# Two-half matmuls on one core: the halves take turns at the accumulation banks

## The chip, the core and the metric

The kernel runs on one core of a Trainium2 chip. The metric is the device time of one execution in microseconds; the median of three runs is given. Engines are named as in the profile: PE (TensorE; PEld its weight loads), DVE (VectorE), ACT (ScalarE), POOL (GpSimd), SP (SyncE, which here issues the transfers).

## The reference, cut to what matters

```python
# 8192 tokens (2 x 4096), 192 features, 8 heads, 7 taps
w = softmax(weight_gen, axis=-1)                  # per token and head
y[s, h] = sum_k w[s, h, k] * x_padded[s + k, h]   # causal convolution
h1 = silu(y @ w_gate) * (y @ w_val)               # 192 -> 1536
z = h1 @ w_out                                    # 1536 -> 192
h2 = z @ w_in                                     # 192 -> 2048
out = (h2 * clip(h2 + 3, 0, 6) / 6) @ w_out2      # 2048 -> 192
```

## The kernel before

The tokens are worked on in 16 tiles of 512. A tile passes four stages: softmax and convolution on DVE and ACT (`conv_items`, whose last sums are lines 360 and 361; for tiles 0 and 1 PE adds the taps, `conv_pe_items`); transposes on PE, which put features on the partitions (`transposes`); the first layer in 12 blocks of 128 hidden columns (kind 1: `m1_in`, `m1_ew`, `m1_out`); and the second layer in 8 blocks of two times 128 (kind 2: `m2_in`, `m2_ew`, `m2_out`). Softmax comes for two tiles at a time. Products of float32 accuracy are made of three: each operand is split into a high and a low part on ACT and DVE (`gsplit`, lines 571 and 666; for transposed input line 526, for a first-layer result lines 584 to 586).

PE's array is used as two halves of 64 rows (`HALVES`), each of which can run a matmul of its own beside the other; two such matmuls are called a pair here. The 192 features are three chunks of 64. In `in_proj` half 0 adds all three chunks into one bank (pg, or the first ph) and half 1 all three into another (pv, or the second ph): 9 pairs. Each half reads the input in its own partitions, so chunks 0 and 1 are needed in both: `s0` holds them, `s1` is a copy with the halves exchanged, made by two transfers (`swap`, line 432), and `s2` holds chunk 2 twice (`double`). A tile's three input tiles come from a ring of four sets (`alloc_split`).

Accumulation uses eight banks: four for in-projections (pool `hp`), which the transposes share, and four (`acc_bank`). The first-layer out-projection of tiles 0 and 1 is five matmuls on the full array, into two banks; for later tiles (`m1_out_halves`) it is five pairs into four banks, two for each half, which the evacuation (`evacuate`, lines 631 to 641) copies and adds. The second-layer out-projection is 16 pairs in four rounds over four banks; the halves work two banks apart, and a bank changes hands behind a mark, a one-element memset on POOL (line 695), which the matmul that takes the bank waits for.

Instructions are issued in the order in which the code is written. Block by block it is: in-projection of block b, out-projection of an earlier block (`pend`, `drain`), elementwise work of block b on ACT and DVE; convolution and weight conversion are filled in between up to a budget in ns (`take`). An evacuation (`urgent`) is put ahead of the next block's elementwise work (`run_urgent`). Tiles 0 and 1 share their first-layer blocks, while the weights are loaded as 64-bit words and converted (`convert_stream`; `i_part` loads a chunk in two transfers of 64 partitions and rounds it in line 255). Then come the first layers of tiles 2 and 3, and from there second layer of tile t and first layer of tile t + 3 in turn. `to_pe(t + 3)`, the wait for the convolution and the transposes, stands in block 4 of a second-layer phase.

## Time and profile before

| | before |
|---|---|
| median of 3 runs | 1319.44 us (1318.07 to 1319.69) |
| profiled execution, its span | 1317.99 us, 1316.2 us |
| PE busy | 1264.0 us, 96% |
| DVE, ACT, POOL busy | 70%, 52%, 4% |
| moved by DMA | 64.01 MB |

The busy shares say which engine is full, and the chain of waits which work, followed back from the end, set it. Windows give the busy time of a stretch, and the timeline the instructions in it, each with the idle time of its engine just before and what ended that. `PE 64*128` marks a matmul on half of the array; starts of the pairs, not their lengths, tell how fast they follow, since they overlap.

### The profile page before, as it was taken

Reading aid. Unit: us, or ns where it says so; the run is one execution under the profiler, and the core shown is the slowest. Engines: PE = TensorE matmul, PEld = TensorE weight load, DVE = VectorE, ACT = ScalarE, POOL = GpSimd, SP = SyncE. Lnnn points to the kernel's source line nnn. Section 1 sums busy time; section 2 is a strip of 40 time slices with the busy share of each in tenths; the row PEclk is TensorE's granted clock in tenths of the full one; section 3 lists DMA queues with packets and bytes.
Section 4 is the critical chain, followed back from the end, with each engine's and each line's share of the span. In section 5 each row is a group of like instructions: output and inputs, shape, how many; then the busy total and the mean of one; then the engine's idle time right before and its main releaser. Section 6 shows DMA issues by size and latency. Waiting matters only on the chain.

```text
span 1316.2 us, 29560 instructions
## 1 busy us (share of the span) xinstructions
PE 1264.0 (96%) x11992; PEld 1085.9 (83%) x11992; DVE 927.3 (70%) x1500; ACT 686.1 (52%) x1204; POOL 48.3 (4%) x515
## 2 busy tenths in 40 slices
PE   5899798999999999999999999999999999999998
PEld 5666576799798897979888798988979898887998
DVE  5797685698677776777767676777767777655655
ACT  3354454566474544646365454746446463644655
POOL 1000000000000000000000000000000000000000
PEclk8899898999999999999999999999999999999999
DMA  9413433011120211212111111201111120110000
GB/s 216 126 25 90 108 104 79 21 47 27 50 50 13 56 37 42 46 43 49 43 33 37 39 42 50 49 14 55 38 47 42 35 50 13 25 38 21 17 2 25
DMA packets 31304, 64.01 MB, mean 49 GB/s; under 512 B 3588, under 2 KB 19970, under 8 KB 31168
## 3 DMA queue, kind: packets, MB, share of 16 engines
q1 hardware_dynamic: 31168, 62.13, 18.1%
q8 instruction: 94, 1.54, 0.5%
q14 instruction: 42, 0.34, 0.1%
HBM read 30.92 MB, written 6.29 MB: 28 GB/s over the span
## 4 chain that ended last, share of the span: by engine, by line
PE 80%; DVE 10%; ACT 4%; issue 3%; DMA 2%; SPq 0%; ACTq 0%; DVEq 0%; POOL 0%; POOLq 0%
PE a L687 19%; PE pv L539 19%; PE ph L539 18%; PE a L622 13%; PE pg L539 8%; DMA s<-s 1%; DVE p L660 1%; DVE p L568 1%; DVE f L204 1%; DVE f L198 1%; DVE s L586 1%; DVE y L639 1%; DVE yb L636 1%; ACT s L584 1%; DVE tmp L326 1%
## 5 line engine op out<-in xcount | busy, mean ns | idle before, releaser
L539 PE MATMUL pg<-s,wi 64*128 64x512 f32 x1728 | 448.8, 401 | 25.3 <-DMA s<-s 17.9
L539 PE MATMUL pv<-s,wi 64*128 64x512 f32 x1728 | 447.2, 400 | 5.5 <-DVE p L568 3.7
L547 ACT ACTIVATE gh<-p 128x512 fp32r<-128x512 f32 x448 | 276.0, 631 | 234.3 <-DVE p L568 163.8
L539 PEld LDWEIGHTS pv<-s,wi 64*128 64x128 f32 x1728 | 316.8, 187 | 66.5 <-DVE p L568 10.6
L539 PEld LDWEIGHTS pg<-s,wi 64*128 64x128 f32 x1728 | 316.9, 187 | 49.5 <-DMA s<-s 15.6
L539 PE MATMUL ph<-s,wi 64*128 64x512 f32 x2304 | 311.2, 395 | 9.9 <-DVE p L660 8.4
L687 PE MATMUL a<-wo,gh 64*128 64x384 f32 x2016 | 304.3, 354 | 0.1
L687 PE MATMUL a<-wo,gl 64*128 64x192 f32 x2016 | 286.6, 247 | 0.0
L539 PEld LDWEIGHTS ph<-s,wi 64*128 64x128 f32 x2304 | 241.0, 184 | 41.7 <-DVE p L660 17.5
L568 DVE TENSOR_TENSOR p<-p,pv 128x512 f32<-128x512 f32 x192 | 131.7, 686 | 150.9 <-ACT p L566 137.6
L687 PEld LDWEIGHTS a<-wo,gh 64*128 64x128 f32 x2016 | 234.4, 184 | 3.7 <-POOL turn L695 1.8
L687 PEld LDWEIGHTS a<-wo,gl 64*128 64x128 f32 x2016 | 234.5, 187 | 1.6
L660 DVE SCALAR_TENSOR_TENSOR p<-p,ph 128x512 f32<-128x512 f32 x256 | 164.1, 682 | 65.8 <-ACT p L657 65.5
L657 ACT ACTIVATE p<-ph,three 128x512 f32<-128x512 f32 x256 | 161.9, 680 | 72.3 <-PE ph L539 69.9
L566 ACT ACTIVATE p<-pg 128x512 f32<-128x512 f32 x192 | 113.7, 592 | 145.4 <-PE pg L539 122.9
L666 DVE TENSOR_TENSOR gl<-p,gh 128x512 fp32r<-128x512 f32 x256 | 166.1, 688 | 25.9 <-ACT gh L547 17.5
L622 PE MATMUL a<-gh,wo 64*128 64x512 f32 x1008 | 182.2, 392 | 0.0
L571 DVE TENSOR_TENSOR gl<-p,gh 128x512 fp32r<-128x512 f32 x192 | 131.9, 687 | 28.8 <-ACT gh L547 28.8
L622 PEld LDWEIGHTS a<-gh,wo 64*128 64x128 f32 x1008 | 124.4, 184 | 23.2
L622 PE MATMUL a<-gl,wo 64*128 64x512 f32 x672 | 143.0, 392 | 0.0
L622 PEld LDWEIGHTS a<-gl,wo 64*128 64x128 f32 x672 | 92.7, 184 | 15.5
L326 DVE TENSOR_TENSOR tmp<-xt,wg 128x768 f32<-128x768 f32 x94 | 89.3, 952 | 3.1 <-DMA xt<-in_x_dram 3.1
(79 smaller groups left out, 657.2 us busy)
## 6 DMA issues: line engine op xcount, KB each, us to landing
s<-s SPq DMA_DIRECT2D x81, 256.0 KB, 3.9
xt<-in_x_dram SPq DMA_DIRECT2D x14, 960.0 KB, 4.7
out_dram<-o SPq DMA_DIRECT2D x15, 384.0 KB, 2.3
s<-s SPq DMA_DIRECT2D x56, 64.0 KB, 3.1
raw<-in_moe_w_in_dram SPq DMA_DIRECT2D x16, 192.0 KB, 4.4
raw<-in_moe_w_out_dram SPq DMA_DIRECT2D x8, 384.0 KB, 3.2
raw<-in_moe_w_out_dram SPq DMA_DIRECT2D x3, 768.0 KB, 8.1
raw<-in_moe_w_gate_dram SPq DMA_DIRECT2D x5, 384.0 KB, 10.0
```

The costliest lines, as they stand in the source:

```text
L198: nc.vector.scalar_tensor_tensor(out=f_int(q), in0=words(q, I32)[:, :, 0], scalar=29, in1=f_int(q), op0=ALU.logical_shift_right, op1=ALU.b ...
L326: nc.vector.tensor_mul(o[:, :n, :].rearrange("p j (h g) -> p j h g", h=H), xt_t[t][:, k:k + n, :].rearrange("p j (h g) -> p j h g", h=H), ...
L539: nc.tensor.matmul(ps[r][:, :N], w[rows, CHUNKS[r][s], a, c], src[1][s][rows, b, :N], start=(i == 0), stop=(i == len(seq) - 1),)
L547: nc.scalar.activation(gh[:, :N], p[:, :N], AF.Copy)
L566: nc.scalar.activation(p[:, :N], pg[:, :N], AF.Silu)
L568: nc.vector.tensor_mul(p[:, :N], p[:, :N], pv[:, :N])
L571: nc.vector.tensor_sub(gl[:, :N], p[:, :N], gh[:, :N].bitcast(F32))
L622: nc.tensor.matmul(ya_t[t][b + r][:, :N], wo1[rows, i, c:c + P], g[0][m][rows, :N], start=first and k in (0, 2), stop=last and k >= 3,)
L657: nc.scalar.activation(q, ph[:, :N], AF.Relu, bias=three)
L660: nc.vector.scalar_tensor_tensor(out=q, in0=q, scalar=6.0, in1=ph[:, :N], op0=ALU.min, op1=ALU.mult)
L666: nc.vector.tensor_sub(gl[:, :N], q, gh[:, :N].bitcast(F32))
L687: ins = nc.tensor.matmul(z[s][:, :w], gb[m][rows, s * P:(s + 1) * P], late["wo2"][rows, blk, :w], start=first and (q, b, m) in ((0, 0, 0), ...
```

## The change

In every two-half projection each half now works alone on a bank, and halfway the two change places. `in_proj` gives each half its part of one product: half 0 holds chunk 0, half 1 chunk 1, both hold chunk 2. Part one is the half's own chunk into its own bank and chunk 2 into the second one of it (6 pairs); part two is its own chunk for the other half's product, into the other's bank (3 pairs), behind a mark on POOL (`Turn`). `s1` and `swap` are gone, and the ring holds five sets of two. Out-projections of earlier blocks stand between the parts (`plan`: `mid`), and part one of block b + 1 follows part two of block b directly (`block`, `begin`); a first-layer out-projection is cut in two stages, with a turn between them, into two banks for every tile (`PAIRS`), and its evacuation has no copies to add. Transposes of tile t + 1 go to the two free `acc_bank`s after block 8 of tile t's first layer (tiles 3 and 5 to 15); those of tile 2, and of tile 4 in block 4 of tile 1's second layer, stay in the in-projection banks. `i_part` loads a chunk in four transfers. `issue` interleaves the two halves' lists by costs in ns.

```diff
-    def i_part(srcs, dst, c0, n):
+    def i_part(wg, a, wv, b, dst, c0, n):
         def load(raw, o):
-            for (w, a), rows in zip(srcs, HALVES):
-                nc.sync.dma_start(
-                    out=raw[rows, o:o + 3 * n].rearrange("p (s n) -> p s n", s=3),
-                    in_=w[:, a:a + n].rearrange("(s p) n -> p s n", p=D2),
-                )
+            r = raw[:, o:o + 3 * n].rearrange("p (s n) -> p s n", s=3)
+            for q, (w, c) in enumerate(((wg, a), (wv, b))):
+                nc.sync.dma_start(out=r[:, q, :], in_=w[0:P, c:c + n])
+                nc.sync.dma_start(out=r[HALVES[q], 2, :], in_=w[P:D, c:c + n])
...
-                    pe_t[t] = [acc_bank(0), acc_bank(1)[:D2]]
+                    pe_t[t] = [acc_bank(0), acc_bank(2)[:D2]]
...
-    free = list(range(4))
+    free = list(range(5))
...
-    def swap(src):
-        s0, s1, _ = src
-        for a, b in (HALVES, HALVES[::-1]):
-            nc.sync.dma_start(out=s1[a].bitcast(F32), in_=s0[b].bitcast(F32))
...
-    def transposes(t):
+    def transposes(t, banks=None):
...
-                swap(src)
-                if t > 0:
-                    double(src)
...
+        if banks is None:
+            banks = [hp.tile([P, MN], F32, tag="h", name=f"b{r}") for r in range(2)]
+        else:
+            banks = [acc_bank(q) for q in banks]
...
-            swap(src)
...
+    class Turn:
+
+        def __init__(self):
+            self.ends, self.mark, self.waited = [], None, False
+        def end(self, ins):
+            self.ends.append(ins.ins.name)
+            if len(self.ends) == 2:
+                m = nc.gpsimd.memset(turn[:1, :], 0.0)
+                for name in self.ends:
+                    tc.add_manual_dep(m.ins, name, SYNC, reason="turns")
+                self.mark = m.ins.name
+        def wait(self, ins):
+            assert self.mark is not None
+            if not self.waited:
+                tc.add_manual_dep(ins.ins, self.mark, SYNC, reason="turns")
+                self.waited = True
+    def push(parts):
+        for r, p in enumerate(parts):
+            lists[r].extend(p)
+            pushed[r] += len(p)
+    def issue(upto):
+        while any(issued[r] < upto[r] for r in range(2)):
+            r = 0 if clock[0] <= clock[1] else 1
+            if not lists[r] or lists[r][0][2] and not lists[r][0][2].mark:
+                clock[r] = max(clock)
+                r = 1 - r
+            ns, f, waits, ends = lists[r].pop(0)
+            ins = f()
+            if waits is not None:
+                waits.wait(ins)
+            if ends is not None:
+                ends.end(ins)
+            clock[r] += ns
+            issued[r] += 1
...
     def in_proj(ps, src, w, c, N):
-        seq = [(s, a, b) for s in (0, 2, 1) for a, b in ((0, 0), (0, 1), (1, 0))]
-        for i, (s, a, b) in enumerate(seq):
-            for r, rows in enumerate(HALVES):
-                nc.tensor.matmul(
-                    ps[r][:, :N], w[rows, CHUNKS[r][s], a, c], src[1][s][rows, b, :N],
-                    start=(i == 0), stop=(i == len(seq) - 1),
-                )
+        s0, s2 = src[1]
+        terms = ((0, 0), (0, 1), (1, 0))
+        turn = Turn()
+        parts = ([[], []], [[], []])
+        for r, rows in enumerate(HALVES):
+            for part, s, x, b in ((0, r, s0, r), (0, 2, s2, r), (1, 1 - r, s0, 1 - r)):
+                for k, (m, l) in enumerate(terms):
+                    start = s == r and k == 0
+                    stop = part == 1 and k == 2
+                    def go(rows=rows, s=s, x=x, b=b, m=m, l=l, start=start, stop=stop):
+                        return nc.tensor.matmul(
+                            ps[b][:, :N], w[rows, s, m, c], x[rows, l, :N], start=start, stop=stop
+                        )
+                    parts[part][r].append([FULL, go, turn if part == 1 and k == 0 else None, None])
+        for r in range(2):
+            parts[0][r][-1][3] = turn
+        return parts
...
+    PAIRS = [((1, 3), (0, 2))[t % 2] for t in range(T)]
...
+    def m1_out(c, t, i, g):
+
         N = sizes[t] * P
         if i == 0:
-            ya_t[t] = [acc_bank(q) for q in range(4)]
+            ya_t[t] = [acc_bank(q) for q in PAIRS[t]]
+        ya, yb = ya_t[t]
+        gh, gl = g[0]
         first, last = i == 0, i == NB1 - 1
-        for k, (b, c, m) in enumerate([(0, 0, 0), (0, D + D2, 0), (2, P, 0), (0, 0, 1), (2, P, 1)]):
+        work = (
+            (ya, ((0, gh), (D + D2, gh), (0, gl))),
+            (yb, ((P, gh), (P, gl))),
+        )
+        turn = Turn()
+        done = when_both(lambda: m1_done(t)) if last else None
+        stages = ([[], []], [[], []])
+        for stage in range(2):
             for r, rows in enumerate(HALVES):
-                nc.tensor.matmul(
-                    ya_t[t][b + r][:, :N], wo1[rows, i, c:c + P], g[0][m][rows, :N],
-                    start=first and k in (0, 2), stop=last and k >= 3,
-                )
-        if last:
-            a0, a1, b0, b1 = (b[:, :N] for b in ya_t.pop(t))
-            src = y_done(t)
-            def evacuate():
-                y1 = rp.tile([P, MN], F32, tag="p", name="y1")[:, :N]
-                yb = rp.tile([P, MN], F32, tag="p", name="yb")[:, :N]
-                nc.scalar.activation(y1, a0, AF.Copy)
-                nc.scalar.activation(yb, b0, AF.Copy)
-                nc.vector.tensor_add(y1, y1, a1)
-                nc.vector.tensor_add(yb, yb, b1)
-                y2 = rp.tile([P, MN], F32, tag="p", name="y2")[:D2, :N]
-                nc.scalar.activation(y2, yb[D2:], AF.Copy)
-                nc.vector.tensor_add(y2, y2, yb[:D2])
-                y_split(y1, y2, src, N)
-            urgent.append(evacuate)
+                y, terms = work[(r + c + stage) % 2]
+                for k, (col, x) in enumerate(terms):
+                    def go(y=y, col=col, x=x, rows=rows, start=first and stage == 0 and k == 0,
+                           stop=last and stage == 1 and k == len(terms) - 1):
+                        return nc.tensor.matmul(
+                            y[:, :N], wo1[rows, i, col:col + P], x[rows, :N], start=start, stop=stop
+                        )
+                    stages[stage][r].append([FULL, go, turn if stage == 1 and k == 0 else None, None])
+                stages[stage][r][-1][3] = done if stage else turn
+        return stages
...
+        def evacuate():
+            h, l = (src[0][:, m, :N] for m in range(2))
+            y2 = rp.tile([P, MN], F32, tag="p", name="y2")[:D2, :N]
+            nc.scalar.activation(h, ya, AF.Copy)
+            nc.scalar.activation(y2, yb[D2:], AF.Copy)
+            nc.vector.tensor_sub(l, ya, h.bitcast(F32))
+            nc.vector.tensor_add(y2, y2, yb[:D2])
+            y_split(y2, src, N)
...
+        order = (1, 0, 3, 2) if t % 2 or t == 0 else (0, 1, 2, 3)
...
+            before, turn = turns[t][(q + 2) % n], Turn()
+            turns[t][q] = turn
+            for r, rows in enumerate(HALVES):
+                s = order[(q + 2 * r) % n]
+                for b, gb in enumerate(g):
+                    for m, w in ((0, 2 * D), (1, D)):
+                        def go(s=s, rows=rows, w=w, x=gb[m], blk=i + b * NP2,
+                               start=first and (q < 2) and (b, m) == (0, 0),
+                               stop=last and q >= 2 and (b, m) == (1, 1)):
+                            return nc.tensor.matmul(
+                                z[s][:, :w], x[rows, s * P:(s + 1) * P],
+                                late["wo2"][rows, blk, :w], start=start, stop=stop,
+                            )
+                        lists2[r].append([
+                            (202, 83)[m], go, before if (b, m) == (0, 0) else None, None
+                        ])
+                lists2[r][-1][3] = done if last and q == n - 1 else turn
...
+    def begin(b):
+        if b not in begun:
+            kind, t, i = blocks[b]
+            begun[b] = (m1_in if kind == 1 else m2_in)(t, i)
+            push(begun[b][1][0])
...
+    def plan():
+
+        mid = [[] for _ in blocks]
+        tail = [[] for _ in blocks]
+        def put(to, b, what):
+            if b < len(blocks):
+                to[b].append(what)
+        kinds = [x[0] for x in blocks]
+        for c, k in enumerate(kinds):
+            if k == 2:
+                put(mid, c + 2, (c, 0))
+            elif kinds[c + 1] == 2:
+                put(tail, c + 1, (c, 0))
+                put(mid, c + 2, (c, 1))
+            elif kinds[c + 2] == 2:
+                put(mid, c + 2, (c, 0))
+                put(tail, c + 2, (c, 1))
+            else:
+                put(mid, c + 2, (c, 0))
+                put(mid, c + 3, (c, 1))
+        return [sorted(x) for x in mid], [sorted(x) for x in tail]
...
+    def block(b, ns, second=False):
+        kind, t, i = blocks[b]
+        begin(b)
+        ps, parts = begun[b]
+        for c, stage in mid[b]:
+            push(out_parts(c, stage))
+        push(parts[1])
+        upto = list(pushed)
+        for c, stage in tail[b]:
+            push(out_parts(c, stage))
+        if not second and b + 1 < len(blocks) and converted(b + 1):
+            begin(b + 1)
+        issue(upto)
...
+                block(b, budget(kind, t, i), ph is phase1 and k == HOOK)
+                b += 1
+                if ph is phase1 and k == len(ph) - 3:
+                    to_pe(2)
+                if kind == 2 and t == 1 and i == 4:
+                    to_pe(4)
+                if kind == 1 and t >= 2 and t != 3 and t + 1 < T and i == 8:
+                    to_pe(t + 1, PAIRS[t + 1])
```

SP at the start of the program, from the second tile's input on (xt: input rows, raw: weight words, s: split input of tile 0); before, then after:

```order
L143 DMA xt_211<-in_x_dram 128x1536
L148 DMA xt_211<-in_x_dram 63x384 x2
L248 DMA raw_247<-in_moe_w_gate_dram 64x3x256
L248 DMA raw_247<-in_moe_w_val_dram 64x3x256
L432 DMA s_230<-s_229 64x1024 x2
L248 DMA raw_262<-in_moe_w_gate_dram 64x3x256
```

```order
L143 DMA xt_217<-in_x_dram 128x1536
L148 DMA xt_217<-in_x_dram 63x384 x2
L249 DMA raw_252<-in_moe_w_gate_dram 128x256
L250 DMA raw_252<-in_moe_w_gate_dram 64x256
L249 DMA raw_252<-in_moe_w_val_dram 128x256
L250 DMA raw_252<-in_moe_w_val_dram 64x256
```

The exchange of tile 0's input is gone from the queue, and the weight words take twice as many issues.

PE in a second-layer block (ph: in-projection bank, a: out-projection bank, gh and gl: high and low part of the hidden columns, s: input of the layer); before, then after:

```order
L539 MATMUL ph<-s_2469,wi_87 128x512 x6
L539 MATMUL ph<-s_2471,wi_87 128x512 x6
L539 MATMUL ph<-s_2470,wi_87 128x512 x6
L687 MATMUL a_5349<-wo_1005,gh 128x384
L687 MATMUL a_5351<-wo_1005,gh 128x384
L687 MATMUL a_5349<-wo_1005,gl 128x192
L687 MATMUL a_5351<-wo_1005,gl 128x192
```

```order
L740 MATMUL a_4489<-wo_1131,gl 128x192
L740 MATMUL a_4487<-wo_1131,gl 128x192
L596 MATMUL ph<-s_2200,wi_87 128x512 x12
L596 MATMUL ph<-s_2201,wi_87 128x512 x6
L740 MATMUL a_4486<-wo_1131,gh 128x384
L740 MATMUL a_4488<-wo_1131,gh 128x384
```

Where 18 matmuls of one block stood together, there are now six of block b's second part and twelve of block b + 1's first part, and the out-projection of an earlier block comes before that block's second part.

DVE where an even tile's convolution ends and its transposed input is split (acc, tmp, sum: convolution; p, pv, gl: first-layer block; s_7610, s_7611: split input; a_7612, a_7613: transposed); before, then after:

```order
L568 TENSOR_TENSOR p<-p,pv 128x512
L360 TENSOR_TENSOR sum<-acc_4747,tmp 128x512
L361 TENSOR_TENSOR sum<-acc_4747,tmp 128x256
L571 TENSOR_TENSOR gl<-p,gh 128x512
L660 SCALAR_TENSOR_TENSOR p<-p,ph 128x512 x2
```

```order
L629 TENSOR_TENSOR p<-p,pv 128x512
L359 TENSOR_TENSOR sum<-acc_6960,tmp 128x512
L360 TENSOR_TENSOR sum<-acc_6960,tmp 128x256
L632 TENSOR_TENSOR gl<-p,gh 128x512
L517 TENSOR_TENSOR s_7610<-a_7612,s_7610 128x4x64
L517 TENSOR_TENSOR s_7610<-a_7613,s_7610 128x4x64
L517 TENSOR_TENSOR s_7611<-a_7612,s_7611 64x2x64 x2
L517 TENSOR_TENSOR s_7611<-a_7613,s_7611 64x2x64 x2
L629 TENSOR_TENSOR p<-p,pv 128x512
```

The sums stand behind a first-layer block's multiply in both; the split of the transposes now follows them at once, ahead of the next block's multiply, and no longer in the second-layer phase behind.

## Rows read from the trace of the kernel before

**Rows 1.** Page, part 1: busy us, share of the span and instructions of each engine.
```profile
PE 1264.0 (96%) x11992; PEld 1085.9 (83%) x11992; DVE 927.3 (70%) x1500; ACT 686.1 (52%) x1204; POOL 48.3 (4%) x515
```

**Rows 2.** Chain of waits in order of time: start us, duration us, engine and group.
```profile
450.23 2.13 PE ph L539 x15
...
454.84 2.11 PE ph L539 x18
456.95 2.25 PE a L687 x32
...
1215.36 2.13 PE ph L539 x15
```

**Rows 3.** Timeline of PE, steady part: start, us, engine, line, out<-in, xcount [idle<-releaser].
```profile
459.00 0.45 PE L496 MATMUL b<-ident,sum 64*128 64x64 f32 x8
...
495.44 1.09 PE L622 MATMUL a<-gh,wo 64*128 64x512 f32 x6
...
498.71 1.09 PE L622 MATMUL a<-gh,wo 64*128 64x512 f32 x6
```

**Rows 4.** Timeline behind a first-layer result, in a second-layer phase.
```profile
525.30 1.27 DVE L660 SCALAR_TENSOR_TENSOR p<-p,ph 128x512 f32<-128x512 f32 x2
...
526.03 0.49 PE L539 MATMUL ph<-s,wi 64*128 64x512 f32 x1 [0.65 <-DVE p L660]
```

**Rows 5.** Timeline of the start: PE, DVE and ACT.
```profile
26.10 0.84 ACT L255 ACTIVATE wi<-f 128x768 fp32r<-128x768 f32 x1 [0.74 <-DVE f L204]
...
33.68 0.79 PE L539 MATMUL pg<-s,wi 64*128 64x512 f32 x1 [9.75 <-DMA s<-s]
...
35.89 0.60 ACT L566 ACTIVATE p<-pg 128x512 f32<-128x512 f32 x1 [8.95 <-PE pg L539]
...
36.52 0.69 DVE L568 TENSOR_TENSOR p<-p,pv 128x512 f32<-128x512 f32 x1 [10.46 <-ACT p L566]
```

**Rows 6.** Windows: us; busy us (x) PE, PEld, DVE, ACT, POOL; clock; DMA share; GB/s.
```profile
75.50:134.00 58.50, 58.50 (x369) 40.73 (x368) 48.12 (x76) 28.25 (x47) 0.00 (x0) 1.00 0.20 58
134.00:164.30 30.30, 21.99 (x133) 15.08 (x133) 18.95 (x33) 12.05 (x25) 0.00 (x0) 0.89 0.45 105
187.20:219.00 31.80, 23.31 (x154) 17.54 (x152) 18.31 (x38) 14.19 (x29) 0.00 (x0) 0.84 0.39 98
```

**Rows 7.** Timeline of PE: first matmuls behind waits, tiles 0 to 3.
```profile
71.85 0.49 PE L539 MATMUL pv<-s,wi 64*128 64x512 f32 x1 [1.94 <-DVE p L568]
...
147.51 0.79 PE L539 MATMUL pg<-s,wi 64*128 64x512 f32 x1 [4.96 <-DMA s<-s]
...
189.69 0.49 PE L539 MATMUL pg<-s,wi 64*128 64x512 f32 x1 [1.77 <-ACT p L566]
...
191.43 0.62 PE L539 MATMUL pg<-s,wi 64*128 64x512 f32 x1
...
191.86 0.63 PE L539 MATMUL pg<-s,wi 64*128 64x512 f32 x1
...
213.75 0.55 PE L539 MATMUL pg<-s,wi 64*128 64x512 f32 x1 [2.18 <-ACT p L566]
```

**Rows 8.** Timeline of a first-layer block, and the convolution's last sums.
```profile
498.47 0.39 PE L539 MATMUL pv<-s,wi 64*128 64x512 f32 x1
...
499.60 0.69 DVE L568 TENSOR_TENSOR p<-p,pv 128x512 f32<-128x512 f32 x1 [1.11 <-ACT p L566]
...
504.94 0.68 DVE L360 TENSOR_TENSOR sum<-acc,tmp 128x512 f32<-128x512 f32 x1
...
505.54 0.42 DVE L361 TENSOR_TENSOR sum<-acc,tmp 128x256 f32<-128x256 f32 x1
```

**Rows 9.** Groups by line: busy us, mean ns of one, idle before and releasers.
```profile
L695 POOL MEMSET turn<- 1x1 f32 x504 | 44.7, 89 | 1244.7 <-PE a L687 1244.6
L526 DVE TENSOR_TENSOR s<-b,s 64x128 fp32r<-64x128 f32 (+1 forms) x84 | 26.8, 333 | 9.0 <-ACT s L521 7.9
```

**Rows 10.** Waits: engine, tile, line, releaser: us in total, times, longest us.
```profile
PEld a L687 <- POOL turn L695: 1.8, 8, 0.3
```

156 lines of the change are left out of this document (62 added, 94 removed).

## Prediction

> **What bounds the kernel now.** I read the page's busy shares first, then the chain of waits, a table of windows, and the timelines of the places where TensorE (PE) stood still. PE is busy for 1264.0 of 1316.2 us [rows 1], so whatever is won must come from its 52 us of idle time, from stretches at the lower clock, or from matmuls that leave the array half used.
>
> The steady part is regular. In the chain of waits the same place of the cycle returns at 450.23 and, ten cycles later, at 1215.36 [rows 2]: 76.51 us per tile. Its parts are eight second-layer blocks of 2.11 us in-projection and 2.25 us out-projection [rows 2], 34.9 us; twelve first-layer blocks of 3.27 us (the out-projections of two blocks in a row start at 495.44 and 498.71, [rows 3]), 39.2 us; and the transposes, 0.45 us [rows 3]. Together 74.5, so **2.0 us of each cycle is waiting**. One such place is in [rows 4]: PE stands from about 525.4 to 526.03, because the ReLU multiply that would free its bank starts only at 525.30, behind the evacuation of a first-layer result.
>
> The irregular part is the first 264 us, with four losses.
> - At 23.9 to 33.68 PE waits 9.75 us for the exchanged copy of the input (s<-s); VectorE (DVE) idles 10.46 us until 36.52 [rows 5].
> - From 75.5 to 134 PE is fully busy, but on 369 matmuls [rows 6]. A block there has 18 half-array and 5 full-array ones, so these are 369/23 = 16.0 blocks of 3.65 us, not 3.27.
> - From 134 to 164.3, where tile 2's input is transposed, the 30.3 us hold 5 in-projections (45 pairs) and 5 out-projections (25 pairs or full matmuls) at 0.233 us each (3.27/14) and the transposes: 16.8 us of work, **13.5 us lost**.
> - From 187.2 to 219, for tile 3, the same work takes 31.8 us: **15.0 us lost**. [Rows 7] show the waits, 4.96 us for s<-s in the one before, 1.77 and 2.18 us for banks here; behind such a wait pairs start 0.43 us apart (191.43, 191.86), and the granted clock of the two windows is 0.89 and 0.84 [rows 6].
>
> **The change part by part.** The sum is made against the profiled execution, 1317.99 us (0.1% under the median of 1319.44).
>
> *A. No exchanged copy at the start.* The instructions on DVE and ScalarE (ACT) stand there in the same order as before. Without the copy, the three own-half pairs and three shared pairs run until 23.9, the mark behind them takes under 0.5 us (see D), and the three crossed pairs, 0.43 us each at the lower clock, end near 25.5. What is late next is ACT: the weight rounding at 26.10, of 0.84 us, stands ahead of the first SiLU [rows 5]. So SiLU 26.9 to 27.5, and the first multiply on DVE at 27.5 instead of 36.52: 9.0 us. From there DVE works almost without a break up to the second tile's input, so the whole gain passes on. Bounds: 10.46 (all of DVE's idle time) and 6 (the weight transfers, now four shorter issues per chunk instead of two, become late). I take **-9**.
>
> *B. Half-array out-projection for tiles 0 and 1.* A block goes from 3.65 to the 3.27 of the steady part: 16 x 0.38 = 6.1 us. Its cover is thin: DVE was busy 48.1 of those 58.5 us [rows 6] and would now have 52.4. Bounds -6 and 0; I take **-4**.
>
> *C. Tile 2's handover.* Its transposes still go to the in-projection banks, so PE waits for the last multiply: the last pair's start to the multiply's start is 1.13 us (498.47 to 499.60, [rows 8]), and its 0.69 us, less the 0.23 us to PE's next slot, gives 1.6. Two of the six transfers are gone, four remain; 1.5 us of that wait stays. The two evacuations behind it cost 0.5 each. DVE had 18.95 us of work in this window [rows 6], which sets a floor a few us above. 16.8 + 1.6 + 1.5 + 1.0 + 3 = 24, **-6** (bounds -9 and -2).
>
> *D. Tile 3's handover, and the new waits between halves.* The transposes of tile 3 go to two free banks three blocks early, so both s<-s waits there and the bank waits go. In their place the transposes wait for the convolution's last sum, which DVE holds behind the block's multiply. After the last pair's start: 1.13 us to the multiply, three steps of 0.60 us (504.94 to 505.54, [rows 8]), the first transposes at 2.9 instead of 0.23; with a half chance of the lower clock behind it (see F) 3.4, and 0.5 for the evacuation. 15.0 - 3.9 = **-11** (bounds -13 and -6). The turns between the halves I cost at nothing: before, 504 marks on GpSimd (POOL), 89 ns each [rows 9] and each asked for one round of out-projection later, made the weight loads wait 1.8 us in total [rows 10]. Such a round is 2.25/4 = 0.56 us [rows 2]. The new turn in an in-projection has at least four matmuls of 0.233 us behind it, 0.93 us, against a matmul that ends 0.39 us after its start; only the two blocks of a cycle with one stage of out-projection between the parts have half of that. Bounds 0 and 0.1 us each.
>
> *E and F. The steady cycle.* The first-layer result now takes two banks: two DVE additions and two ACT copies of the evacuation go, and the in-projection's banks no longer serve the transposes. Following [rows 4]'s chain with DVE steps of 0.65 us, from the last out-projection: copies until 1.6, subtraction and addition until 2.5, ACT 3.1, DVE 3.8, ReLUs until 4.4, multiplies until 5.1, and PE wants the second bank at 5.2 (3 + 6 pairs, 2.25, 3 pairs). So the lead has shrunk (PE begins a block's first part before the previous out-projection), but it suffices. Of the 2.0 us I leave 0.25: 12 tiles x 1.75 = **-21**, and **-1** for tile 3's own result (bounds together -25 and -8).
> But the transposes of tile t+1 now stand in first-layer block 8 of tile t, behind that block's in-projection. The convolution has from one second-layer phase to here; where a softmax comes first (tiles 6, 8, 10, 12, 14), its last sum stands behind block 8's multiply, as the order shows. Since PE works in order, everything waits: 1.13 + 2 x 0.60 us to the end of the sum, then 0.42 us for the second sum and the transposes: they end near 2.9 instead of 0.6, 2.3 us each. Idle times of this size left the clock up once (1.94 us) and brought it down twice (1.77 and 2.18 us) [rows 7]; a fall costs about eight pairs 0.19 us more each, 1.5 us. With half of that: 5 x 3.05 = **+15** (bounds +11 and +19). For the odd tiles the sum is two blocks early and costs nothing. Behind the transposes follow, in block 9, six ACT copies and six DVE subtractions of 0.33 us [rows 9] ahead of its SiLU and multiply, and four transfers on SP (six before); the multiply comes up to 2.0 us later, and its bank is wanted a whole block (3.27 us) after the next in-projection begins, so they cost nothing; without that cover, 1 us per tile.
>
> Sum: -9 - 4 - 6 - 11 - 21 - 1 + 15 = -37: 1318 - 37 = **1281 us**.
>
> **The rivals.**
> *The lead is too short.* Elementwise work gets 4.36 us in a second-layer block from the end of an in-projection to the reuse of its bank, where it had 6.6 (4.36 + 2.25). Against it: both multiplies end 2.5 us after the last pair starts; for it: DVE is nearly full in the early tiles, and urgent evacuations come in bunches. If half of C and F's gain goes that way, -37 + 3 + 10 = -24, and with more falls of the clock -20: 1296 to 1300.
> *More is gained.* No fall of the clock at the sums, and B and C at their ends: 1270.
> *The copies were covered.* If the weights' transfers, not the copy, set the start and the early tiles stay bound by DVE, A to D vanish, and -7 is left of the sum, or -3 with the clock falling at each of the five sums: 1311 to 1315. Against it: DVE idled 10.46 us in that very wait.
> *The turns are exposed (slower).* Each in-projection has one new wait on the way of both halves, since PE is one queue: 320 blocks (16 x 20). It decides from 37/320 = 0.12 us each; with the mean of the eight waits on a mark that the trace has, 1.8/8 = 0.23 us [rows 10], at every block it is 72 us: 1353. For it: two engines are crossed at each turn. Against it: those eight are all that 504 marks caused. The Trainium skill (page "TensorE: Matmul & The Clock Gate", section "The cost: per-tile semaphore tail") says that completion increments of packed tiles serialize behind the last matmul, 25 + 4.7 per tile + 26.3 ns per increment; an estimate from it for two tiles and two increments is 0.09 us per turn, which by that rule, were it exposed at 320 in-projections and 192 out-projections, would give 1281 + 45 = 1326. The trace does not show such a tail on the path at the turns it has.
>
> **How the numbers follow.** Forecast 0.60; short lead 0.18; more gained 0.08; covered copies 0.06; exposed turns 0.08. A measurement here tells about 0.2%, 2.6 us, from no change. Faster: 0.60 + 0.18 + 0.08 + a little of the fourth, 0.87 (its 1315 is within 0.2% or near it); same 0.04; slower 0.09. The range runs from A to F near their lower bounds, 1266, into the short-lead case, 1302.
>
> **What would show it.** Right: the first multiply near 27.5 us; the first-layer out-projections of tiles 0 and 1 in 3.3 us steps; no s<-s among PE's waits before 150 us but a short one for tile 2; a cycle of 75 us for odd tiles, and 77 to 79 for those five where PE waits on the sum. Wrong: PE waiting on POOL turn for more than a few us, pairs further apart than 0.235 us at full clock, or banks released late in every block.

## The result, and the profile after

The changed kernel takes 1299.09 us, the median of four runs (1298.69 to 1300.22), against 1319.43 us: a ratio of 0.9849 (95% interval 0.9832 to 0.9866). The range of the prediction, 1266 to 1302, held it; the predicted time, 1281 us, is 18 us too low, and half of the forecast gain did not come. The spans of the two profiled executions, 1316.2 and 1297.5 us, differ by 18.7 us, and the readings below account for that difference.

Part 1 of the page of the changed kernel answers to [rows 1]:

```profile
PE 1253.9 (97%) x12112; PEld 1137.8 (88%) x12112; DVE 908.7 (70%) x1473; ACT 680.5 (52%) x1177; POOL 93.0 (7%) x1012
```

A kernel of numbered blocks is compared best by one instruction that each block has once. Here that is the elementwise multiply on DVE (line 568 or 660 before, 629 or 708 after): the same block's multiply in both traces, and the difference of the two starts. It grows to -9.4 us at the first block, shrinks to -4.4 by the third, and is -7.6 just ahead of tile 2's transposes, -15.1 at tile 2's third block and -21.3 us at the first second-layer block. There it stays: at the last tile it is -21.0, and the end of the program gives 2.3 us back. **The whole gain lies in the first 230 us; the steady part, where 7 us were expected, gained nothing.**

The steady part in the timeline of DVE, changed kernel: the first multiply of the second block of the second layer of tiles 3, 4 and 5 (start, duration, engine, line, operation).

```profile
428.08 0.69 DVE L708 SCALAR_TENSOR_TENSOR p<-p,ph 128x512 f32<-128x512 f32 x1
...
502.99 0.69 DVE L708 SCALAR_TENSOR_TENSOR p<-p,ph 128x512 f32<-128x512 f32 x1
...
581.74 0.69 DVE L708 SCALAR_TENSOR_TENSOR p<-p,ph 128x512 f32<-128x512 f32 x1
```

One cycle lasts 74.91 us, the next 78.75; before they lasted 76.40 and 76.63 (the same instruction at 448.90, 525.30 [rows 4] and 601.93). A cycle without an even tile's transposes wins 1.5 to 1.7 us, and one with them loses 2.1 to 2.4 (0.9 in the one of the five behind whose wait the clock stayed up). What the long one has in it is to be seen in the timeline of PE and DVE at 404 us:

```profile
404.63 0.69 DVE L629 TENSOR_TENSOR p<-p,pv 128x512 f32<-128x512 f32 x1 [0.88 <-ACT p L627]
405.24 0.69 DVE L359 TENSOR_TENSOR sum<-acc,tmp 128x512 f32<-128x512 f32 x1
...
405.84 0.42 DVE L360 TENSOR_TENSOR sum<-acc,tmp 128x256 f32<-128x256 f32 x1
...
406.07 0.68 PE L487 MATMUL a<-ident,sum 64*128 64x64 f32 x8 [1.99 <-DVE sum L359]
...
408.94 0.62 PE L596 MATMUL pg<-s,wi 64*128 64x512 f32 x1
...
409.37 0.50 PE L670 MATMUL a<-gh,wo 64*128 64x512 f32 x2
```

PE stands for 1.99 us until the sum behind the multiply is there, and then works at the lower clock. The windows of 8 us around the five waits (us, busy time of PE, PEld, DVE, ACT and POOL with counts, granted clock, DMA share, GB/s) show the clock:

```profile
403.00:411.00 8.00, 6.01 (x47) 5.25 (x45) 4.89 (x12) 2.85 (x8) 0.18 (x2) 0.79 0.31 115
556.70:564.70 8.00, 6.01 (x47) 5.00 (x45) 4.87 (x12) 2.85 (x8) 0.18 (x2) 0.79 0.31 114
710.20:718.20 8.00, 6.00 (x47) 5.12 (x45) 4.82 (x12) 2.85 (x8) 0.18 (x2) 0.79 0.28 107
864.10:872.10 8.00, 6.01 (x61) 4.73 (x59) 4.96 (x13) 3.45 (x9) 0.27 (x3) 1.00 0.31 115
1016.00:1024.00 8.00, 5.99 (x47) 4.80 (x45) 4.88 (x12) 2.85 (x8) 0.18 (x2) 0.79 0.32 118
```

The wait is the same in all five, 6.0 of 8 us busy; in four the clock is at its lower level for a part of the window (mean 0.79) and PE gets 47 matmuls done, in one it stays up and PE does 61.

At the start the page's chain of waits (start, duration, what) and the timeline show a second place. PE is held by the first block's out-projection, which waits for weights that ACT and DVE still have to round, and tile 1's taps, 80 matmuls, are queued behind it:

```profile
33.71 0.50 PE L670 MATMUL a<-gh,wo 64*128 64x512 f32 x1 [3.34 <-ACT wo L272]
36.69 0.76 PE L670 MATMUL a<-gh,wo 64*128 64x512 f32 x1 [2.47 <-DVE wo L239]
```

```profile
39.70 11.13 PE a L400 x80
```

```profile
27.10 0.69 DVE L629 TENSOR_TENSOR p<-p,pv 128x512 f32<-128x512 f32 x1 [1.40 <-ACT p L627]
...
50.47 0.69 DVE L474 TENSOR_TENSOR s<-a,s 128x512 fp32r<-128x512 f32 x1 [5.16 <-ACT s L468]
```

So DVE, which had its first multiply 9.4 us earlier than in [rows 5], idles 5.16 us for tile 1's transposed input, where it idled 1.88 us before. The lead at the third block differs from one execution to the next: it is 2.9 to 4.4 us in the six profiled executions, this one and five of those below, that share the code of this stretch.

### The profile page after: what moved, and what is told of

Same layout as the page of the kernel before. It is cut to its first block, busy times and chain, and to the rows that moved or that the text cites. A ratio compares the mean times of both kernels' runs of the same rounds, so it can differ in the third digit from the quotient of the medians.

```text
span 1297.5 us, 30233 instructions
## 1 busy us (share of the span) xinstructions
PE 1253.9 (97%) x12112; PEld 1137.8 (88%) x12112; DVE 908.7 (70%) x1473; ACT 680.5 (52%) x1177; POOL 93.0 (7%) x1012
## 4 chain that ended last, share of the span: by engine, by line
PE 88%; DVE 6%; ACT 3%; DMA 2%; issue 1%; SPq 0%; POOL 0%; DVEq 0%; ACTq 0%; POOLq 0%
PE a L740 22%; PE ph L596 21%; PE pg L596 16%; PE a L670 15%; PE pv L596 12%; DVE p L629 1%; PE a L400 1%; ACT p L627 1%; DVE f L204 1%; DMA raw<-in_moe_w_val_dram 1%; DVE f L198 1%; DMA raw<-in_moe_w_gate_dram 1%; PE a L487 0%; PE a L755 0%; DVE gl L632 0%
## 5 line engine op out<-in xcount | busy, mean ns | idle before, releaser
L596 PEld LDWEIGHTS pg<-s,wi 64*128 64x128 f32 x1728 | 302.6, 186 | 28.7 <-ACT p L627 5.5
L670 PE MATMUL a<-gh,wo 64*128 64x512 f32 x1152 | 258.4, 397 | 5.8 <-ACT wo L272 3.3
L740 PE MATMUL a<-wo,gl 64*128 64x192 f32 x2016 | 259.6, 248 | 0.1
L596 PEld LDWEIGHTS ph<-s,wi 64*128 64x128 f32 x2304 | 224.9, 184 | 36.5 <-POOL turn L539 3.1
L670 PE MATMUL a<-gl,wo 64*128 64x512 f32 x768 | 215.5, 396 | 0.8 <-DVE gl L632 0.8
L740 PEld LDWEIGHTS a<-wo,gl 64*128 64x128 f32 x2016 | 198.3, 187 | 6.7 <-DVE gl L714 1.9
L740 PEld LDWEIGHTS a<-wo,gh 64*128 64x128 f32 x2016 | 195.8, 184 | 7.1 <-POOL turn L539 1.3
L670 PEld LDWEIGHTS a<-gh,wo 64*128 64x128 f32 x1152 | 169.9, 187 | 16.5 <-ACT wo L272 3.8
L539 POOL MEMSET turn<- 1x1 f32 x1001 | 89.3, 89 | 1176.2 <-PE ph L596 260.9
L670 PEld LDWEIGHTS a<-gl,wo 64*128 64x128 f32 x768 | 122.0, 187 | 8.5 <-DVE gl L632 1.8
```

The costliest lines, as they stand in the source:

```text
L539: m = nc.gpsimd.memset(turn[:1, :], 0.0)
L596: return nc.tensor.matmul(ps[b][:, :N], w[rows, s, m, c], x[rows, l, :N], start=start, stop=stop)
L670: return nc.tensor.matmul(y[:, :N], wo1[rows, i, col:col + P], x[rows, :N], start=start, stop=stop)
L740: return nc.tensor.matmul(z[s][:, :w], x[rows, s * P:(s + 1) * P], late["wo2"][rows, blk, :w], start=start, stop=stop,)
```

## The experiments

All of them start from the changed kernel, 1299.1 us. The kernel before took 1318.6 to 1319.9 us beside them. Executions of one kernel lie up to 5 us apart (1294.43 to 1299.30 us in the first run on the evacuation below), so a gain of 2 or 3 us in a median alone shows little; the traces say where it was won.

**The order at the start.**

```diff
+        mid[HOOK].remove((0, 0))
+        mid[HOOK + 1].append((0, 0))
         return [sorted(x) for x in mid], [sorted(x) for x in tail]
```

> The changed kernel with one thing moved: the out-projection of the very first block is issued one block later, behind the 80 matmuls that add tile 1's taps, instead of ahead of them. Nothing is left out. Theory (PE's order at the start eats half of the gain): in the changed kernel PE stands still 3.34 and 2.47 us for that block's weights, from 30.4 to 36.7 us, with the tap matmuls queued behind it, which so end at 50.8; now they start near 33 and end near 47.5, DVE's wait of 5.16 us falls under 2, and everything behind comes 3 to 4 us earlier: 1295 to 1296 us. Rival (the weights' four transfers per chunk, or the doubled split of chunk 2 on ACT and DVE, set this place): the taps still end after 50 us, and the time moves by less than 1 us from 1299.1.

Measured: 1295.98 us. In the timeline of DVE the wait is 1.88 us again, and the split of tile 1's input starts at 46.72 instead of 50.47:

```profile
46.72 0.69 DVE L474 TENSOR_TENSOR s<-a,s 128x512 fp32r<-128x512 f32 x1 [1.88 <-ACT s L468]
```

The third block's multiply comes 3.7 us earlier, and 2.9 us of that last to the end. PE's order was the cause of the larger part. The traces also show where the rest of 1.3 us lies: from the start of that split to the third block's multiply it is 3.03 us here (46.72 to 49.75), 3.02 in the changed kernel and 1.62 before (56.25 to 57.87). ACT and DVE now split the second half of chunk 2 themselves, where a transfer doubled it; the step on DVE, in the kernel before and in this run:

```profile
57.26 0.68 DVE L485 TENSOR_TENSOR s<-a,s 64x512 fp32r<-64x512 f32 x1 [0.32 <-ACT s L479]
```

```profile
48.34 1.38 DVE L476 TENSOR_TENSOR s<-a,s 64x512 fp32r<-64x512 f32 x2 [0.92 <-ACT s L470]
```

**The transposes and the sum.**

```diff
-                if kind == 1 and t >= 2 and t != 3 and t + 1 < T and i == 8:
+                if kind == 1 and t >= 2 and t != 3 and t + 1 < T and i == (10 if t % 2 else 8):
```

> The changed kernel with the transposes of the tiles 6, 8, 10, 12 and 14 (and those of tile 4 as before) put two blocks later, behind first-layer block 10 instead of 8; the convolution stays where it was. Nothing is left out. Theory (PE waits there for the convolution's last sum, and the clock falls behind the wait): the five cycles of 78.75 us become the 74.9 us of the others, 4 x 3.84 + 2.3 = 17.7 us: 1281 to 1282 us, with no wait of PE on the sum and no fall of the clock in the steady part. Rival (the excess is the evacuation of the transposes on ACT and DVE, which delays SiLU and multiply wherever it stands): the cycles stay above 77 us and the time above 1294 us.

Measured: 1282.83 us (ratio to before 0.9716, interval 0.9694 to 0.9738), 16.3 us less than the changed kernel. Every cycle from tile 2's on now lasts 74.5 to 75.2 us (the instruction shown above stands at 425.34, 500.25 and 575.16), none has a wait on the sum, and the same five windows are full at the full clock, two of which are:

```profile
403.00:411.00 8.00, 8.00 (x72) 8.00 (x70) 5.16 (x9) 3.10 (x5) 0.44 (x5) 1.00 0.37 125
...
864.10:872.10 8.00, 8.00 (x71) 7.63 (x69) 6.49 (x13) 5.11 (x11) 0.44 (x5) 1.00 0.18 36
```

The evacuation of the transposes was not moved away, only two blocks on, so the rival that blamed it is out. Against these cycles, a wait costs 3.84 us where the clock falls behind it, and 2.3 where it does not.

**The place of the transposes itself.**

```diff
+                if kind == 2 and t >= 1 and t + 3 < T and i == 4:
+                    to_pe(t + 3)
-                if kind == 2 and t == 1 and i == 4:
-                    to_pe(4)
-                if kind == 1 and t >= 2 and t != 3 and t + 1 < T and i == 8:
+                if kind == 1 and t == 2 and i == 8:
                     to_pe(t + 1, PAIRS[t + 1])
```

> The changed kernel with the transposes of the tiles 4 to 15 where they were before the change: in two in-projection banks, behind block 4 of a second-layer phase. Those of tiles 2 and 3 stay. Nothing is left out. Theory (what the move of the transposes was for shows only if they also keep clear of the sum): the five waits on the sum go, 17.7 us, and each of the 11 phases has a wait of 1.2 us for in-projection banks as tile 4's has at 283 us: some 1299 - 17.7 + 11 = 1292 us. Rival (with a wait of 1.2 us in every cycle and the clock falling behind some of them, the old place costs as much as the new one): 1299 us. Other rival (the wait is made up inside the phase): 1284 us.

Measured: 1306.24 us, worse than every branch: 23.4 us behind the version with the later transposes, 2.1 us for each of 11 tiles. The timeline of PE shows the expected wait of 1.20 us in each phase; in the new order it is not made up again, and the block behind it comes 2.4 us later, against the block ahead of it, than in the changed kernel. Why a wait of 1.2 us costs more than itself was not followed up.

```profile
518.19 1.09 PE L596 MATMUL ph<-s,wi 64*128 64x512 f32 x3 [1.20 <-DVE p L708]
```

With the new order, then, the free banks are worth 2.1 us a tile, if the transposes come when the sum is there; in block 8 the even tiles gave more than that back.

**Half-array or full array for tiles 0 and 1.** The five pairs of `m1_out` become five full matmuls for t < 2, in the order of the kernel before:

```diff
+        if t < 2:
+            for k, (y, col, x) in enumerate((
+                (ya, 0, gh), (ya, D + D2, gh), (yb, P, gh), (ya, 0, gl), (yb, P, gl)
+            )):
...
+                    ins = nc.tensor.matmul(
+                        y[:, :N], wo1[:, i, col:col + P], x[:, :N],
```

> The changed kernel with the first-layer out-projection of tiles 0 and 1 on the full array as before: five matmuls per block instead of five pairs in two turns. Nothing is left out. Theory (the half-array form is worth what it saves on PE where PE sets the pace): the multiplies between 80 and 124 us step by 3.65 instead of 3.3 us, and 3 to 6 us are lost: 1302 to 1305 us. Rival (DVE sets the pace there, and the gain seen in that stretch came from the missing copies): the steps stay, 1299 us.

Measured: 1306.43 us. The windows from 84 to 126 us, this kernel first and the changed kernel below it (columns as above):

```profile
84.00:126.00 42.00, 42.00 (x269) 29.55 (x271) 33.06 (x50) 18.84 (x32) 1.47 (x11) 1.00 0.20 62
```

```profile
84.00:126.00 42.00, 39.08 (x339) 30.78 (x337) 36.13 (x59) 21.18 (x36) 2.49 (x23) 1.00 0.26 79
```

With full matmuls PE is busy without a gap and the multiplies step by 3.66 us (85.47, 89.19, 92.79, 96.46); with pairs PE has 2.9 us of slack and DVE does more in the same time. From the third block to 126 us the full form loses 5.7 us, as the theory has it, though the whole time is above its range. Another 4 us come at tile 2's handover, of which 1.5 are left from its third block on. The granted clock is 0.86 there (126 to 150 us) and 1.00 in the changed kernel (121 to 145), but that does not explain them: the run with the late transposes has 0.86 in that window too and loses nothing.

**The evacuation ahead of a SiLU.** In the changed kernel's trace PE waits 2.82 us where tile 3 begins, for a SiLU that stands behind four steps of an evacuation (timeline):

```profile
193.49 0.58 ACT L685 ACTIVATE s<-a 128x512 fp32r<-128x512 f32 x1
194.09 0.59 ACT L686 ACTIVATE y<-a 64x512 f32<-64x512 f32 x1
...
195.43 0.63 ACT L644 ACTIVATE s<-y 64x512 fp32r<-64x512 f32 x1 [0.75 <-DVE y L688]
196.09 0.60 ACT L627 ACTIVATE p<-pg 128x512 f32<-128x512 f32 x1
...
196.74 0.73 PE L596 MATMUL pg<-s,wi 64*128 64x512 f32 x3 [2.82 <-ACT p L627]
```

```diff
+        first = (t, i) == (3, 0)
+        if not first:
+            run_urgent()
...
         nc.vector.tensor_mul(p[:, :N], p[:, :N], pv[:, :N])
+        if first:
+            run_urgent()
```

> The changed kernel with SiLU and multiply of tile 3's first block issued ahead of the evacuation of tile 2's first-layer result, on ACT and DVE, instead of behind it. Nothing is left out. Theory (the lead that an in-projection now has is too short for an evacuation of 2.6 us ahead of its SiLU at the one place where a first layer follows a first layer): PE's wait of 2.82 us at 196.7 goes, and with it the fall of the clock behind it, 1.5 us: 1295 us. Rival (DVE and ACT are full there with weight conversion, and the wait moves to the next block): less than 1 us.

Measured: 1297.13 us in the median and 1297.5 us in the span, as the changed kernel; the wait is still there, 2.81 us. This run did not test the theory: the evacuation stands ahead of the third block, since tile 2's last out-projection stage is issued with it, and all that moved is one SiLU, ahead of two steps of weight conversion on ACT. It is so nearly a second measurement of the changed kernel. The next one names that block, `(t, i) == (3, 2)`.

> The changed kernel with SiLU and multiply of tile 3's third block issued ahead of the evacuation of tile 2's first-layer result: that evacuation stands ahead of the third block, not of the first as the run before this one had it. Nothing is left out. Theory (the lead is too short for an evacuation ahead of a SiLU at this one place): PE's wait of 2.82 us at 196.7 goes, and the fall of the clock behind it, 1.5 us: 1295 us. Rival (DVE and ACT have too much to do there, and the wait moves on): less than 1 us.

Measured: 1296.12 us. The wait goes, the multiply comes 3.8 us earlier, but 0.61 and 0.81 us of waiting appear at the out-projection behind it, and in the trace 2.1 to 2.4 us are left of the 4.3. Theory and rival each have half of it; the medians (1296.12 against 1297.13 us in the run before) could not tell.

**Tile 3's transposes.**

```diff
-                if kind == 1 and t >= 2 and t != 3 and t + 1 < T and i == 8:
+                if kind == 1 and t >= 2 and t != 3 and t + 1 < T and i == (9 if t == 2 else 8):
```

> The changed kernel with the transposes of tile 3 behind first-layer block 9 of tile 2 instead of block 8; the convolution stays where it was. Nothing is left out. Theory (tile 3's handover was sized too well because PE waits on the sum for as long as in the steady cycles): the wait of 2.85 us at 165.4 goes, 1296 us. Rival (the splits of the transposed input, later by one block, now delay the first in-projections of tile 3, which follow two blocks behind): 1299 us or more.

Measured: 1298.64 us, no difference. The wait of 2.85 us on the sum is gone, and two others are in its place, for a multiply and for a transfer of the split input (timeline of PE):

```profile
178.58 0.49 PE L596 MATMUL pv<-s,wi 64*128 64x512 f32 x1 [0.94 <-DVE p L629]
...
180.31 0.50 PE L596 MATMUL pg<-s,wi 64*128 64x512 f32 x1 [1.00 <-DMA s<-s]
```

The time is the rival's, though not by the splits' lateness alone: one of the two waits is for a multiply. In this stretch DVE has 27.6 us of work in 36 (164 to 200 us), and a wait that is taken away comes back elsewhere. What was won is hidden besides by the clock: in the changed kernel's profiled execution it stayed up behind the wait of 2.85 us, while in the run with the late transposes it fell behind the same wait (2.87 us at 168.4) and the next multiply came 2.6 us later.

**The turns.** Four more memsets behind every mark, one more behind every mark, and four more behind the marks of the in-projections alone:

```diff
+                for _ in range(4):
+                    m = nc.gpsimd.memset(turn[:1, :], 0.0)
                 self.mark = m.ins.name
```

> The changed kernel with every mark on POOL followed by four more memsets, the last of which is the one waited for: each of the 1001 turns comes 4 x 0.09 = 0.36 us later, or more. Nothing is left out. Theory (the turns are hidden, with some 0.5 us to spare in an in-projection and 0.2 us in a round of the second layer's out-projection, 0.56 less 0.35 for the last matmul and 0.09 for the mark): the in-projections lose nothing; the rounds lose up to 0.2 us each, at 504 rounds at most 100 us, and if they too have more room, nothing. Rival (turns are on the path already, and part of the gain that did not come went to them): every turn loses 0.36 us, 360 us, or at the 320 in-projections alone 115 us.

> The changed kernel with one more memset behind every mark, 0.09 us for each of 1001 turns. Nothing is left out. Theory (a round of the second layer's out-projection has about 0.14 us to spare, the four extra memsets of 0.36 us having cost 0.9 us per block of four rounds): within 3 us of 1299. Rival (the rounds have nothing to spare, and the turns were part of the gain that did not come): 504 x 0.09 = 45 us more, 1344 us.

> The changed kernel with four more memsets behind the mark of every in-projection only (320 marks); those of the out-projections stay as they were. Nothing is left out. Theory (the in-projection's turn has four or more matmuls behind it and 0.5 us to spare, and the loss of the run with longer marks came from the rounds of the second layer's out-projection): below 1306 us, at most 7 us lost, in the blocks that have one stage of out-projection between the parts. Rival (the in-projection's turn is on the path and was part of the 0.9 us that each second-layer block lost there): 0.2 to 0.36 us for each of 320, 1363 us or more.

Measured: 1438.98, 1309.57 and 1342.78 us. Each memset takes 0.15 us of POOL's time, not 0.09 (the four together 0.53, the mark and its four 0.73), so the marks came 0.58 and some 0.15 us later. In the first run most of the waits on a mark sit in the second layer's rounds (waits: engine, tile, line, releaser; us in total, times, longest us):

```profile
PEld a L742 <- POOL turn L543: 91.8, 129, 1.0
PE a L742 <- POOL turn L543: 61.8, 126, 0.8
```

The third run shows how one kind of mark delays another. In the timeline of POOL, the mark of a round has to pass the four memsets of an in-projection's mark, since POOL is one queue:

```profile
522.49 0.09 POOL L539 MEMSET turn<- 1x1 f32 x1 [2.02 <-PE ph L598]
522.63 0.53 POOL L543 MEMSET turn<- 1x1 f32 x4
523.22 0.09 POOL L539 MEMSET turn<- 1x1 f32 x1
523.60 0.09 POOL L539 MEMSET turn<- 1x1 f32 x1 [0.29 <-PE a L742]
```

A second-layer block lasts 4.49 us in this run (PE's in-projections start at 520.09 and 524.58) and 4.36 in the changed kernel (508.32 and 512.68). Over 128 blocks these 0.13 us are 17 of the 44 us lost, and there PE waits for the mark of a round that came late (the next round's first matmul starts at 523.36, behind the mark of 523.22) and not for the in-projection's own.

All three of my numbers were wrong: the longer marks cost 140 us where 100 was the most, those of the in-projections alone 44 us and not 7, and one more memset 10.5 us and not 3. None of the rivals came either (360 or 115 us lost, 1363 and 1344 us). What a turn costs in the changed kernel as it is can be read from its own waits, 6.8 us in all for 1001 marks:

```profile
PEld ph L596 <- POOL turn L539: 3.1, 13, 0.2
...
PEld pv L596 <- POOL turn L539: 1.9, 3, 0.7
...
PEld a L740 <- POOL turn L539: 1.3, 6, 0.2
```

(and 0.5 us for two matmuls). The turns are hidden, but by a margin of the order of a single memset of 0.15 us.

**All together.** The moves of the runs on the start, the late transposes (tile 3 one block, even tiles two), the evacuation, and at the end of the program:

```diff
+        for s in range(sizes[t]):
+            for i, g in rest[:-1]:
+                m2_out_last(t, i, g, s)
         for s in range(sizes[t]):
-            for i, g in rest:
+            for i, g in rest[-1:]:
                 m2_out_last(t, i, g, s)
```

> The changed kernel with four moves of order together: the first block's out-projection behind tile 1's taps, the transposes of even tiles two blocks later and those of tile 3 one block later, SiLU and multiply of tile 3's third block ahead of the evacuation, and at the end of the program all of the next to last block's out-projection ahead of the last one's, so that PE does not wait 1.77 us for the last high part. Nothing is left out. Theory (the losses are separate places on PE's way and add up): 3.0 + 16.6 + 2.9 + 4.3 + 2 to 3 us, 1269 to 1271 us. Rival (a gain of one place is given back at the next, in the stretch up to 230 us where DVE is over 75% busy): 1274 us or more.

Measured: 1271.71 us (ratio to before 0.9641, interval 0.9626 to 0.9657), faster than both kernels and just above the theory's range. By the multiplies' starts 5.4 us were won up to the first second-layer block, where the theory has 10.2, so the rival is half right there; 17.7 us were won in the steady part, and 4.4 behind the last multiply, more than expected. Of the changed kernel, timeline: PE waits there for the last high part, and the outputs then follow 2.1 us apart; the window's clock is 0.68.

```profile
1286.42 0.44 PE L755 MATMUL a<-wo,gh 128*128 128x384 f32 x1 [1.77 <-ACT gh L607]
...
1288.73 0.36 DVE L761 SCALAR_TENSOR_TENSOR o<-a,lo 128x192 f32<-128x192 f32 x1 [1.04 <-ACT lo L760]
...
1290.87 0.36 DVE L761 SCALAR_TENSOR_TENSOR o<-a,lo 128x192 f32<-128x192 f32 x1 [1.77 <-ACT lo L760]
```

```profile
1286.00:1297.50 11.50, 7.53 (x28) 6.95 (x28) 3.02 (x7) 2.29 (x6) 0.00 (x0) 0.68 0.11 34
```

With all four moves the same window is at the full clock:

```profile
1260.00:1270.10 10.10, 6.34 (x42) 4.97 (x38) 4.01 (x8) 3.82 (x8) 0.09 (x1) 1.00 0.13 40
```

The clock is the larger part of this difference, and the move did not buy it. The first run on the evacuation has the end of the changed kernel, with the same wait, and there the clock stayed up:

```profile
1289.11 0.44 PE L759 MATMUL a<-wo,gh 128*128 128x384 f32 x1 [1.78 <-ACT gh L607]
```

```profile
1288.50:1297.50 9.00, 4.76 (x28) 4.03 (x28) 3.22 (x7) 2.48 (x6) 0.00 (x0) 1.00 0.14 44
```

From the start of the last multiply to the end it takes 9.19 us there, 11.91 in the changed kernel's profiled execution and 7.49 with all four moves. So the move itself is worth 1.7 us, about the wait that it takes away, and 2.7 are a fall of the clock that not every execution has.

## Why the prediction was right in its range and wrong in its size

| term | predicted | measured, by the multiplies' starts |
|---|---|---|
| A, start | -9 | -9.4 at the first multiply, -4.4 at the third |
| B, half-array form, tiles 0 and 1 | -4 | -3.2 in its stretch; 5.7 lost there when undone |
| C, tile 2's handover | -6 | -7.5 |
| D, tile 3's handover | -11 | -6.3 |
| E and F, steady gain | -22 | -17.6 (11 cycles of 1.6) |
| F, sums of five even tiles | +15 | +17.7 (four of 3.84, one of 2.3) |
| end of the program | 0 | +2.3 (-0.4 where the clock stayed up) |
| sum | -37 | -19 |

- **A, mis-sized: the step "so the whole gain passes on".** The first multiply came at 27.10 us, where 27.5 was forecast. I had compared DVE's and ACT's order, which is the same in both kernels but for the second half of chunk 2, and not PE's: the out-projection of block 0 had moved ahead of the taps. The first run gives back 3.7 us of the 5.1 that were lost, and the split of chunk 2 has the rest. The reason given for the lower bound, late weight transfers, was not the mechanism: between 27 and 50 us no wait of DVE is for a transfer.
- **B, right in mechanism.** Where PE set the pace the multiplies step by 3.0 to 3.5 us, and PE gets slack. The cover was as thin as said: DVE is busy 36.1 of 42 us there. That this is why 3.2 and not 6.1 us came is argued and not shown; undoing the form cost 5.7 us where it had won 3.2, and the 2.5 between them are open.
- **C, right in its sum, by luck in its parts.** PE waited 2.83 us at 123.8 and not 1.6, and not for the last multiply, which was only starting, but for the last SiLU, which stood behind a step of weight conversion on ACT (timeline below). The wait on the split input was 2.15 us at 130.0, against 1.5. The clock stayed up (1.00 from 121 to 145 us, 0.89 in [rows 6]), but that is not what paid for the longer waits: in the run with the late transposes it is 0.86 in the same window, second below, and the handover gains the same 7.5 us. Which part was shorter than forecast stays open.

```profile
122.77 0.52 ACT L254 ACTIVATE wi<-f 128x384 fp32r<-128x384 f32 x1 [0.94 <-DVE f L204]
123.20 0.58 ACT L627 ACTIVATE p<-pg 128x512 f32<-128x512 f32 x1
123.81 0.69 DVE L629 TENSOR_TENSOR p<-p,pv 128x512 f32<-128x512 f32 x1 [1.07 <-ACT p L627]
123.83 0.46 PE L487 MATMUL b<-ident,sum 64*128 64x64 f32 x7 [2.83 <-ACT p L627]
```

```profile
121.00:145.00 24.00, 18.86 (x159) 15.50 (x160) 19.96 (x37) 12.37 (x26) 0.89 (x10) 1.00 0.24 61
121.00:145.00 24.00, 20.89 (x156) 18.59 (x158) 19.97 (x37) 12.38 (x26) 0.89 (x10) 0.86 0.24 60
```

- **D, mis-sized: the 0.5 us for the evacuation.** The wait on the sum was 2.85 us (timeline of PE below), about as worked out. The evacuation of tile 2's result cost 2.82 us and a fall of the clock: the chain of copies, subtraction and addition ahead of an elementwise step was counted for the steady cycle only, where PE has the out-projection in between. Moving it won back 2.1 to 2.4 us of the 4.7 that were missing; the rest is not located. In three more executions with this order (the runs with the late transposes, with the transposes back, and the first on the evacuation) the clock fell behind the wait on the sum too, and D was worth 4.8 to 5.2 us.

```profile
168.29 0.46 PE L487 MATMUL a<-ident,sum 64*128 64x64 f32 x8 [2.85 <-DVE sum L359]
```

- **E and F, right in mechanism.** A cycle without the waits is 74.91 us where 75 was forecast; in the steady part the waits on the sum came at those five tiles and no others, 78.75 us (77 to 79 forecast). The clock fell behind four of the five, not half. Terms of almost equal size and opposite sign (-17.6 and +17.7) made the steady part worth nothing; I expected -7.
- **The end** was in no term. PE waits 1.77 us there, and in this execution the clock fell behind it; where it stayed up, with the same wait, the end is 0.4 us shorter than before (9.19 against 9.62 us from the last multiply). So the +2.3 is the fall, not the order.

So the forecast time missed by 18 us while its terms for the steady part held, and that the range took the result in is owed in part to the width given to it for a rival, the short lead. That rival named the right time, 1296 to 1300, by another way than the kernel took: its mechanism appears at one place of the program (2.82 us), and not in the steady cycles. By its own sums, -24 to -20 from 1318, it should have said 1294 to 1298. The exposed turns did not come: 6.8 us of waits on marks, 6.3 of them of weight loads, which is more than the few us given as a sign of being wrong and still about 0.5% of the time. The estimate from the Trainium skill (page "TensorE: Matmul & The Clock Gate", section "The cost: per-tile semaphore tail"), 45 us if every turn's tail were exposed, is not borne out by the trace; but the run with one more memset per mark shows that the cover is thin.

## What to carry to other kernels

When a change moves one engine's order, compare the order on every engine that others wait for, here PE at the start: equal orders on DVE and ACT say nothing of a matmul that waits at the head of PE's queue with work behind it that others need. Put a step that needs another engine's last result (the transposes, the final out-projection) where that result is a block old, and not where free banks come first: 16 us lay in a distance of two blocks. Before a gain is put down to a move, see whether the clock fell at that place in other executions of the same order: 2.7 of the 4.4 us at the end were the clock's. Where many handovers share one queue for their marks, count the marks' time on that queue as well as the latency of each.

## What the runs showed of the hardware that I had not expected

A wait of 1.99 us brought PE's clock down to 1.2 GHz four times out of five in the profiled execution of the changed kernel (windows above, mean granted clock 0.79 of 8 us), and the same wait left it at 2.4 GHz the fifth time; in the runs that kept the five waits, which of them escaped differed (the one at 865 us here, the one at 402 us in the run with the evacuation behind the third block's SiLU), and in the run with tile 3's transposes later none did. A fall cost 1.5 us each time (3.84 against 2.3 us). A memset of one element on POOL is shown as 0.09 us, but back to back they follow 0.15 us apart (five in 0.73 us).
